# The steps of an expert layer without a copy for changing weights: only the conversion stands in branches

## The chip, the cores and the metric

The kernel runs on one core of a Trainium2 chip. The metric is the time of the whole program on the device in microseconds (us). Three runs of the kernel before gave 1397.78, 1398.32 and 1402.83 us; their median is 1398.32. The profile was taken from one more execution.

The engines are TensorE (PE; its weight loads are listed as PEld), VectorE (DVE), ScalarE (ACT), GpSimd (POOL) and SyncE (SP). Each has its own stream of instructions with its own branches; semaphores order them between engines. A "q" behind an engine's name (PEldq, ACTq) marks what its sequencer does itself: loads of registers, branches, and the issue of transfers.

## The reference, cut to what matters

```python
attn_out = _attn_ref(**attn_kwargs)              # 8 x 8 heads, 576 positions in chunks of 64, softmax per chunk
x = attn_out.transpose(0, 2, 1, 3).reshape(B * S, H * D)     # 4608 tokens x 512
h = np.maximum(x @ w_in, 0.0)                    # dense layer, 512 -> 2048 -> 512
x = (h * h @ w_out).astype(np.float32)
# _moe2_ref: one of 8 experts for each token, 512 -> 1024 -> 512
logits = x @ w_gate + modality_bias[modality_id]
e_idx = np.argmax(logits, axis=1)
probs = softmax(logits)
for e in range(E):
    mask = e_idx == e
    h = np.maximum(x[mask] @ w1[e], 0.0)
    out[mask] = probs[mask, e, None] * (h @ w2[e])
```

All arrays are fp32. The change concerns the last part alone, the layer of experts. With these inputs the router uses two of the eight experts, 2 and 3, for 2325 and 2283 tokens.

## The kernel before, in words

The kernel goes through attention, the dense layer and the layer of experts in one program. It writes each fp32 number as the sum of two f16 numbers (high and low) and leaves out the product of the two low parts, so each matrix product is three matmul passes.

For the layer of experts, the tokens are sorted by expert and cut into pairs of two tiles of 128 tokens; a pair belongs to one expert. There are places for 25 pairs (`PAIRS`); here 19 are used, 0 to 9 for expert 2 and 10 to 18 for expert 3. `NP` is 18 and `EARLY` is 4. Each pair's two matrix products are done by a scheme with seven products of quarter size. `pair1(p)` makes the seven products with w1: 24 matmuls of 128x128 each (L952), into four banks of PSUM in the order a, c, b, a, c, d, a. Each is moved out behind its matmuls by `pair_c`, on ACT (line 90 is the helper of all ACT operations) and DVE (line 93 is the helper of scalar_tensor_tensor). `pair2(p)` makes the seven products with w2: 12 matmuls of 128x256 each (L1018); `pair_o` scales by the gate's weight and `put` (L1044) writes rows of the output by an indirect DMA on POOL. Between its products `pair_s` makes the sums of pair p+1's hidden values for the next `pair2`, split into f16 (L991 to L1003 and L93).

The tokens of a pair come in three operations: `x_gather` (indirect DMA on POOL, L854), `x_tr` (two transposing DMAs, issued from ACT's queue for pairs from 4 on, L862), and `x_sum0` / `x_sum1` (sums by DVE L881, POOL L884 to L887 and L896).

The weights of the current expert stand in SBUF in seven blocks per matrix, each as high and low f16 (`WB`). To make new ones, `load_raw` brings 2 MB of fp32 to the tile `raw` (SP, L773), `presum` scales them on ACT and makes four sums on DVE and POOL (L803), and `conv_part` makes the high part on ACT and the low part on DVE (L824; on POOL for the blocks 2, 4 and 6). Whether a transfer is done is a register's value: with 0 the instruction is issued and moves nothing.

A table of flags in SBUF (`changes`; tiles `chga` and `chgb`) tells for each pair whether its expert is another than that of the pair before. In step p, which is `pair1(p+1)` and then `pair2(p)`, each engine loads a flag to a register and branches. If neither pair p nor p+2 has a new expert, it runs one copy of the step (`fast`); otherwise another (`slow`), which has inside two further choices, between a `first` that converts new w2 between its products and one that doesn't, and likewise a `second` for new w1. So the program of each step holds up to five versions of its halves. In this run the slow copy is taken in steps 8 and 10; new raw weights are loaded in steps 7 and 9, w1 for step 8 and w2 for step 10. Pairs 18 and on may not exist, so the step 17 is inside another branch, `tail`, whose other side is the last `pair2`.

The order of the instructions on each engine is the order in which this code is written.

## Time and profile before

| | |
|---|---|
| median of three runs | 1398.32 us |
| profiled execution | 1397.62 us |
| span in the profile, first to last instruction | 1395.9 us |
| mean granted clock of TensorE | 0.95 |
| TensorE matmul busy | 1231.3 us, 88% of the span |
| VectorE busy | 863.3 us, 62% |
| ScalarE busy | 661.5 us, 47% |
| GpSimd busy | 671.1 us, 48% |

The first matmul of step 2 starts at 953.14 us, the last matmul ends at about 1390 us. So the part which the change touches is some 440 us, the last third of the span. The shares of busy time are means over the whole program; in that third TensorE's are lower.

In a row of the timeline the first number is the start, the second how long the row's instructions took, then the engine, the line, what it writes and reads, how many there are, and in square brackets how long the engine had stood idle before and what released it. "issue" there is time in which the engine waited for nothing that the profile shows.

### The profile page before, as it was taken

What the parts mean: (1) busy time and instruction counts of PE and PEld (TensorE: products, weight loads), DVE (VectorE), ACT (ScalarE), POOL (GpSimd) and SP (SyncE); (2) the same over time, 40 slices, a digit from 0 to 9 for tenths busy, and PEclk for the clock granted to TensorE, in tenths of its full rate; (3) what the DMA queues carried; (4) which work ended last, traced back from release to release, by engine and by line L of the source; (5) the groups of instructions that cost most, each with busy time, mean ns of one, the idle gap of its engine ahead of it and who ended that gap; (6) DMA issues with size and microseconds to landing.
All of it is one profiled execution on the core that took longest, in us unless ns stands there. A gap on an engine that the chain in (4) does not pass through costs nothing. (4 is left out here: it accounts for less than half of the span.)

```text
span 1395.9 us, 30217 instructions
## 1 busy us (share of the span) xinstructions
PE 1231.3 (88%) x12045; PEld 771.2 (55%) x12045; DVE 863.3 (62%) x1787; ACT 661.5 (47%) x1212; POOL 671.1 (48%) x593
## 2 busy tenths in 40 slices
PE   4998999999999999999999987687897745888895
PEld 3444444444444444444444435367787745787784
DVE  6898866746648467474672466765565464655653
ACT  6886644635436345263462443334444344544442
POOL 4476442613416135043250376663665474666664
PEclk9999999999999999999999998889999887999998
DMA  9364323134233232432312043402324315224341
GB/s 373 118 198 126 91 61 92 46 80 73 69 82 63 69 84 52 85 62 61 77 24 46 24 121 91 91 18 62 73 71 132 71 40 87 48 62 80 64 95 34
DMA packets 146161, 115.13 MB, mean 82 GB/s; under 512 B 119770, under 2 KB 119806, under 8 KB 145938
## 3 DMA queue, kind: packets, MB, share of 16 engines
q1 hardware_dynamic: 104514, 83.28, 22.9%
q0 software_dynamic: 7632, 20.54, 4.9%
q10 hardware_dynamic: 33792, 8.39, 4.6%
q8 instruction: 132, 2.16, 0.7%
q14 instruction: 91, 0.75, 0.2%
HBM read 140.10 MB, written 19.80 MB: 115 GB/s over the span
## 5 line engine op out<-in xcount | busy, mean ns | idle before, releaser
L510 PE MATMUL hp<-xtall,big 128*128 128x512 f16 x1728 | 390.6, 383 | 0.0
L525 PE MATMUL op<-big,big 128*128 128x512 f16 x1728 | 387.1, 382 | 0.5 <-POOL big L490 0.5
L525 PEld LDWEIGHTS <-big 128*128 128x128 f16 x1728 | 165.8, 99 | 195.1 <-issue 6.2
L510 PEld LDWEIGHTS <-big 128*128 128x128 f16 x1728 | 165.2, 98 | 194.0 <-issue 8.0
L952 PEld LDWEIGHTS <-big 128*128 128x128 f16 x3192 | 205.3, 106 | 99.5 <-issue 77.3
L490 POOL TENSOR_TENSOR big<-g,big 128x512 f16<-128x512 f32 x144 | 178.3, 1242 | 138.0 <-DVE g L93 94.2
L952 PE MATMUL hq<-big,big 128*128 128x128 f16 x2040 | 142.2, 236 | 86.2 <-issue 29.6
L590 POOL DMA_INDIRECT meta<-mt,di x36 | 37.0, 1027 | 317.2 <-issue 198.1
L93 DVE SCALAR_TENSOR_TENSOR g<-r,bq 128x512 f32<-128x512 f32 x138 | 137.6, 999 | 52.5 <-ACT r L90 44.7
L90 ACT ACTIVATE r<-hp 128x512 f32<-128x512 f32 x138 | 81.8, 593 | 112.9 <-PE hp L510 92.4
L90 ACT ACTIVATE big<-r,bls 128x512 f16<-128x512 f32 x138 | 99.4, 721 | 5.5 <-DVE bls L99 0.6
L1018 PEld LDWEIGHTS <-xtall 128*128 128x128 f16 x840 | 83.8, 100 | 27.0 <-issue 15.5
L1018 PE MATMUL oq<-big,xtall 128*128 128x256 f16 x600 | 74.7, 283 | 12.9 <-DVEq L1376 8.1
L1018 PEld LDWEIGHTS <-ho 128*128 128x128 f16 x756 | 74.9, 100 | 15.4 <-issue 6.0
L90 ACT ACTIVATE xs<-op 128x512 bf16<-128x512 f32 x36 | 21.3, 592 | 122.0 <-PE op L525 122.0
L90 ACT ACTIVATE xtall<-cq 128x512 f16<-128x512 f32 x70 | 42.9, 626 | 66.1 <-DVE cq L93 26.2
L1018 PE MATMUL oq<-big,ho 128*128 128x256 f16 x540 | 65.9, 279 | 5.8 <-DVE oo L93 5.8
L1044 POOL DMA_INDIRECT out_dram<-oo,tib x30 | 34.0, 1135 | 75.6 <-POOLq L1381 42.4
L90 ACT ACTIVATE ho<-cq 128x512 f16<-128x512 f32 x63 | 38.7, 626 | 65.5 <-DVE cq L93 26.2
L90 ACT ACTIVATE big<-hq 128x512 f32<-128x512 f32 x56 | 32.0, 593 | 78.3 <-PE hq L952 32.9
L968 DVE TENSOR_TENSOR cq<-s_all,big 128x512 f32<-128x512 f32 x19 | 13.1, 690 | 79.0 <-ACT big L90 39.5
L90 ACT ACTIVATE ee<-ee 128x512 f32<-128x512 f32 x36 | 22.4, 624 | 78.8 <-DVE ee L332 78.7
(284 smaller groups left out, 1907.7 us busy)
## 6 DMA issues: line engine op xcount, KB each, us to landing
raw<-in_w_dram SPq DMA_DIRECT2D x38, 2048.0 KB
qk<-in_qk_dram SPq DMA_DIRECT2D x36, 512.0 KB
vv<-in_v_dram SPq DMA_DIRECT2D x36, 256.0 KB
x2d<-xs SPq DMA_DIRECT2D x36, 256.0 KB
big<-in_w_in_dram SPq DMA_DIRECT2D x16, 512.0 KB
raw<-in_w_out_dram SPq DMA_DIRECT2D x16, 512.0 KB
raw<-in_w_dram SPq DMA_DIRECT2D x8, 512.0 KB
x2t<-xs SPq DMA_TRANSPOSE x36
```

The source lines that it names most:

```text
L90: nc.scalar.activation(out=out, in_=in_, func=func, **kw)
L93: nc.vector.scalar_tensor_tensor(out=out, in0=in0, scalar=s, in1=in1, op0=op0, op1=op1, **kw)
L490: nc.gpsimd.tensor_tensor(out=lo, in0=q32.rearrange("p (f n) -> p f n", f=nf), in1=hi, op=ALU.subtract)
L510: nc.tensor.matmul(hp[:, q_ * n:(q_ + 1) * n], lhsT=wi[:, la, kk, f * 128:f * 128 + 128], rhs=x[:, lb, kk, :], start=i == 0, stop=i == 3 * ...
L525: nc.tensor.matmul(ps, lhsT=g[:, la, f, t * 128:t * 128 + 128], rhs=wo[:, lb, f, :], start=f == 0 and n == 0, stop=f == KF - 1 and n == 2)
L590: nc.gpsimd.indirect_dma_start(out=meta[:, :], out_offset=bass.IndirectOffsetOnAxis(ap=di[:, 0:1].bitcast(U32), axis=0), in_=mt, in_offset ...
L952: nc.tensor.matmul(ps[:, f * 128:f * 128 + 128], lhsT=WB[0][:, n, la, kk, f * 128:f * 128 + 128], rhs=xa(lb, kk), start=first and f + m + ...
L968: tt(out=c11, in0=bk["b"], in1=SN[0], op=ALU.add)
L1018: nc.tensor.matmul(ps, lhsT=hb[:, la, f * 128:f * 128 + 128], rhs=WB[1][:, n, lb, f, :], start=first and f + m == 0, stop=True, skip_group ...
L1044: nc.gpsimd.indirect_dma_start(out=out[:, :], out_offset=bass.IndirectOffsetOnAxis(ap=t.bitcast(U32), axis=0), in_=o, in_offset=None, boun ...
```

## The change

The step has one version. TensorE's matmuls, and what the other engines do for the tokens, stand in one line of code; between its products are two points. At `point_a`, between the third and fourth product of `pair1(p+1)`, and at `point_b`, between the fourth and fifth product of `pair2(p)`, each engine loads a flag (`gA`, `gB`) and skips the point if nothing is to be done there. Inside stand the conversions alone, under flags of their own: the sums of new w1 at `point_a` of the step in which they were in line before, their conversion at `point_b` of it; the sums of new w2 at `point_b` of the step ahead, their conversion at `point_a`. Behind each point SP issues three conditional loads of raw weights. The table of flags has 13 rows in place of 5. In the tail, the side that goes on behind step 17 is laid out so that the end of the program for 19 pairs comes right behind it.

```diff
@@ -720,20 +720,39 @@
+    ROWS = ("e", "n", "gA", "gB", "sA1", "sA0", "sB0", "sB1", "E1", "E2b", "M1", "E2", "L2")
+
     def changes(n, name):
...
+        put_row("gA", sh[0], sh[2], ALU.max)
+        put_row("gB", sh[1], sh[2], ALU.max)
...
+        put_row("M1", sh[3], t0, ALU.mult)
+        put_row("E2", t0, sh[3], ALU.is_gt)
         return rg
@@ -777,13 +796,13 @@
         load_raw(x, e, part)
 
     def steer(p, row):
-        return mp["rg", int(row == 4 or p >= EARLY)][0:1, row, p:p + 1]
-
-    def late_raw(x, p, which=1):
+        return mp["rg", int(("rg", 1) in mp)][0:1, ROWS.index(row), p:p + 1]
+
+    def late_raw(x, p, row, at):
         if p >= PAIRS:
             return
-        e = nc.sync.value_load(steer(p, 0), min_val=0, max_val=E - 1)
-        need = nc.sync.value_load(steer(p, which), min_val=0, max_val=1)
+        e = nc.sync.value_load(steer(p, "e"), min_val=0, max_val=E - 1)
+        need = nc.sync.value_load(steer(at, row), min_val=0, max_val=1)
         load_raw(x, e, cond=need, cond_hint=False)
 
     def halves(x, v, k):
@@ -826,8 +845,7 @@
     def late_sums(x):
         mp["sums", x] = presum(x, extras(x), [nc.vector, nc.gpsimd, nc.gpsimd, nc.vector])
 
-    def late_both(x):
-        late_sums(x)
+    def late_conv(x):
         for n in range(7):
             conv_part(x, n, mp["sums", x])
 
@@ -1341,106 +1359,103 @@
             fn(*a)
         T = TEND
 
-        def pair1(p, part=range(7), src=None, early=False):
+        def pair1(p, part=range(7), src=None):
             nonlocal T
             for n in part:
                 flush(T)
                 pair_mm1(p, n)
                 if src is not None:
-                    for k in ((0, 1, 2), (3, 4), (5, 6), (), (), (), ())[n] if early else [n]:
+                    for k in ((0, 1, 2), (3, 4), (5, 6), (), (), (), ())[n]:
                         conv_part(1, k, src)
                 pair_c(p, n)
                 T += 1.33
 
-        def pair2(p, part=range(7), s=None, src=None):
+        def pair2(p, part=range(7), s=None):
             nonlocal T
             for n in part:
                 flush(T)
                 pair_mm2(p, n)
-                if src is not None:
-                    conv_part(0, n, src)
                 pair_o(p, n)
-                if s is not None and src is None:
+                if s is not None:
                     pair_s(s, n)
                 T += 1.33
-            if s is not None and src is not None and 6 in part:
-                for n in range(7):
-                    pair_s(s, n)
 
         def branch(p, row):
             on = nc.values_load(steer(p, row), min_val=0, max_val=1)
             return tc.If(on > 0, preferred_fallthrough_block=False)
 
-        def when(p, fn, *a):
-            if p < PAIRS:
-                with branch(p, 1):
-                    fn(*a)
-
-        def both(p, row, yes, no):
-            was = set(gone)
-            with branch(p, row) as cond:
-                yes()
-            after = set(gone)
-            gone.clear()
-            gone.update(was)
-            with cond.Else():
-                no()
-            assert gone == after
-
-        def first(p, src=None):
+        def when(p, row, fn, *a):
+            with branch(p, row):
+                fn(*a)
+
+        def point_a(p):
+            def inner():
+                if p + 1 < PAIRS:
+                    when(p, "sA1", late_sums, 1)
+                when(p, "n", late_conv, 1)
+                if p + 2 < PAIRS:
+                    when(p, "sA0", late_sums, 0)
+
+            when(p, "gA", inner)
+
+        def loads_a(p):
+            late_raw(0, p + 2, "sB0", p)
+            late_raw(0, p + 3, "E1", p)
+            late_raw(1, p + 1, "E2b", p)
+
+        def point_b(p):
+            def inner():
+                if p + 2 < PAIRS:
+                    when(p, "sB0", late_sums, 0)
+                    when(p + 2, "n", late_conv, 0)
+                if p + 1 < PAIRS:
+                    when(p, "sB1", late_sums, 1)
+
+            when(p, "gB", inner)
+
+        def loads_b(p):
+            late_raw(0, p + 3, "M1", p)
+            late_raw(1, p + 2, "E2", p)
+            late_raw(1, p + 1, "L2", p)
+
+        def step(p):
             once(x_tr, p + 2)
-            pair1(p + 1, src=src)
+            pair1(p + 1, range(3))
+            point_a(p)
+            loads_a(p)
+            pair1(p + 1, range(3, 7))
             once(x_gather, p + 3)
             once(x_sum0, p + 2)
-
-        def second(p, src=None):
-            if src is None:
-                pair2(p, range(4), p + 1)
-                late_raw(1, p + 1)
-                late_raw(0, p + 3, 2)
-                once(x_sum1, p + 2)
-                pair2(p, range(4, 7), p + 1)
-            else:
-                pair2(p, range(3), p + 1, src)
-                once(x_sum1, p + 2)
-                pair2(p, range(3, 7), p + 1, src)
-                late_raw(1, p + 1)
-                late_raw(0, p + 3, 2)
-
-        def fast(p):
-            first(p)
-            second(p)
-
-        def slow(p):
-            def new2():
-                late_sums(1)
-                first(p, mp["sums", 1])
-
-            def new1():
-                late_sums(0)
-                second(p, mp["sums", 0])
-
-            both(p, 1, new2, lambda: first(p))
-            late_raw(0, p + 2, 3)
-            if p + 2 < PAIRS:
-                both(p + 2, 1, new1, lambda: second(p))
-            else:
-                second(p)
-
-        def step(p):
-            both(p, 4, lambda: slow(p), lambda: fast(p))
+            pair2(p, range(4), p + 1)
+            point_b(p)
+            loads_b(p)
+            once(x_sum1, p + 2)
+            pair2(p, range(4, 7), p + 1)
+
+        def last(p):
+            def ready():
+                when(p, "sA1", late_sums, 1)
+                late_conv(1)
+
+            when(p, "n", ready)
+            pair2(p)
+
+        def first_change():
+            late_sums(0)
+            late_conv(0)
 
         once(x_gather, 2)
         once(x_gather, 3)
-        pair1(1, src=mp["pre"], early=True)
+        pair1(1, src=mp["pre"])
         once(x_tr, 2)
         once(x_tr, 3)
-        late_raw(0, 2, 2)
+        late_raw(0, 2, "n", 2)
+        late_raw(0, 3, "E1", 0)
         once(x_sum0, 2)
         pair2(0, range(4), 1)
         extras(0)
-        when(2, late_both, 0)
-        late_raw(0, 3, 2)
+        when(2, "n", first_change)
+        loads_b(0)
         once(x_sum1, 2)
         pair2(0, range(4, 7), 1)
         once(x_sum0, 3)
@@ -1450,9 +1465,15 @@
         pair1(2)
         flush(T + 30.0)
         assert not ev
-        when(3, late_both, 0)
-        late_raw(1, 2)
-        late_raw(0, 4, 2)
+
+        def second_change():
+            when(1, "sA0", late_sums, 0)
+            when(3, "n", late_conv, 0)
+            when(1, "sB1", late_sums, 1)
+
+        when(1, "gB", second_change)
+        late_raw(0, 4, "E1", 1)
+        loads_b(1)
         once(x_gather, 4)
         for n in range(7):
             pair_s(2, n)
@@ -1462,15 +1483,13 @@
 
         def tail(p):
             if p == PAIRS - 1:
-                when(p, late_both, 1)
-                pair2(p)
+                last(p)
                 return
-            with tc.If(n_pairs > p + 1 - EARLY) as cond:
+            with tc.If(n_pairs > p + 1 - EARLY, preferred_fallthrough_block=p == NP - 1) as cond:
                 step(p)
                 tail(p + 1)
             with cond.Else():
-                when(p, late_both, 1)
-                pair2(p)
+                last(p)
 
         tail(NP - 1)
```

On ACT, the border between two steps. `cq` holds the quarters of the hidden values, `ho` their f16 parts, `ms` scaled output, `hq` the first products of the next pair. Before:

```order
L90 ACTIVATE ho_11185<-cq_11417 128x512 [waits DVE_49]
L90 ACTIVATE ms<-rq,fsa 128x256 [waits PE_49]
L90 ACTIVATE ho_11186<-cq_11418 128x512 [waits DVE_49]
L90 ACTIVATE ho_11188<-cq_11419 128x512 [waits Pool_49]
L1381 UNCONDITIONAL_BRANCH [waits Activation_sequencer_49]
L1371 TENSOR_LOAD chga
L1381 COMPARE_AND_BRANCH
L862 DMA_TRANSPOSE big_94<-big_94 128x8x128 [waits DMAHW4_49,DMAHW3_49,DMAHW5_49,DMAHW2_49,DMAHW7_49,DMAHW1_49,DMASW2_49]
L862 DMA_TRANSPOSE big_94<-big_94 128x8x128 [waits DMASW3_49]
L90 ACTIVATE big_92<-hq_11390 128x512 [waits PE_49]
```

And now:

```order
L90 ACTIVATE ms<-rq,fsa 128x256 [waits PE_49]
L90 ACTIVATE ho_11196<-cq_11428 128x512 [waits DVE_49]
L90 ACTIVATE ho_11198<-cq_11429 128x512 [waits Pool_49]
L880 DMA_TRANSPOSE big_94<-big_94 128x8x128 [waits DMAHW5_49,DMASW4_49]
L880 DMA_TRANSPOSE big_94<-big_94 128x8x128 [waits DMAHW6_49,DMASW5_49]
L90 ACTIVATE big_92<-hq_11400 128x512 [waits PE_49]
L90 ACTIVATE big_92<-hq_11401 128x512 [waits PE_49]
L90 ACTIVATE xtall<-cq_11427 128x512 [waits DVE_49]
L1384 TENSOR_LOAD chgb
L1388 COMPARE_AND_BRANCH
L1388 UNCONDITIONAL_BRANCH [waits Activation_49,Activation_sequencer_49]
```

The flag and the branch that stood between the last `ho` and the two transposes are gone from there; a flag and a branch now stand behind the first `xtall` of the next pair (point a).

On PE, the border between the last product of `pair2` (`rq`, `oq` of `xtall` here) and the first of the next `pair1` (`hq`). Before:

```order
L1018 LDWEIGHTS xtall
L1018 MATMUL oq_12105<-big_93,xtall 128x256
L1381 UNCONDITIONAL_BRANCH [waits PE_sequencer_49]
L1371 TENSOR_LOAD chga
L1381 COMPARE_AND_BRANCH
L952 LDWEIGHTS big_92 [waits DMAHW3_49,Activation_49]
L952 MATMUL hq_11390<-big_94,big_92 128x128 [waits DVE_49]
L952 LDWEIGHTS big_92
```

And now:

```order
L1036 LDWEIGHTS xtall
L1036 MATMUL oq_12134<-big_93,xtall 128x256
L970 LDWEIGHTS big_92 [waits DMAHW5_49,Activation_49]
L970 MATMUL hq_11400<-big_94,big_92 128x128 [waits DVE_49]
L970 LDWEIGHTS big_92
```

The branch between the two steps is gone, and the weight load of the next pair follows the last matmul.

On PE, between the third product (`s_all`) and the fourth (`hq`) of `pair1`, where nothing but matmuls stood before, there is now:

```order
L970 LDWEIGHTS big_92
L970 MATMUL s_all<-big_94,big_92 128x128
L1384 TENSOR_LOAD chgb
L1388 COMPARE_AND_BRANCH
L1388 UNCONDITIONAL_BRANCH [waits PE_sequencer_49]
L1384 TENSOR_LOAD chgb [waits DVE_49]
L1388 COMPARE_AND_BRANCH
```

The last row is the way past the point; it waits for the engine's own sequencer. The conversion has no matmul, so the skipped code of PE holds flags and branches alone.

## Rows read from the trace of the kernel before

**Rows 1.** Windows by step: start and end, length, busy us of engines, PEclk, DMA.
```profile
982.16:1004.32 22.16, 18.88 (x253) 17.56 (x253) 13.48 (x20) 10.40 (x19) 14.35 (x13) 1.00 0.32 75
1070.74:1103.64 32.90, 22.13 (x252) 20.81 (x253) 16.32 (x23) 11.70 (x21) 16.95 (x15) 0.81 0.51 130
1103.64:1134.18 30.54, 23.16 (x252) 20.76 (x253) 15.06 (x13) 18.20 (x26) 17.94 (x13) 0.86 0.21 40
1134.18:1184.26 50.08, 22.58 (x253) 21.13 (x252) 28.06 (x31) 17.57 (x28) 28.82 (x22) 0.75 0.44 87
1184.26:1205.31 21.05, 20.00 (x252) 18.89 (x253) 17.93 (x17) 12.70 (x20) 14.13 (x10) 0.94 0.10 28
1205.31:1232.85 27.54, 20.36 (x254) 18.91 (x252) 16.48 (x20) 12.26 (x23) 19.49 (x18) 0.94 0.24 59
1232.85:1258.07 25.22, 21.52 (x253) 20.19 (x253) 13.38 (x19) 10.52 (x19) 14.85 (x13) 0.86 0.34 66
1325.63:1348.43 22.80, 20.34 (x252) 19.15 (x253) 13.60 (x20) 10.47 (x20) 14.62 (x13) 0.93 0.31 73
```

**Rows 2.** Timeline of step 12's second half and step 13's start.
```profile
1268.84 2.78 PE L1018 MATMUL oq<-big,ho 128*128 128x256 f16 x24
...
1271.80 1.01 POOL L884 TENSOR_TENSOR big<-big 128x256 f32<-128x256 f32 x1 [1.01 <-DVE big L881]
...
1278.69 1.53 DVE L93 SCALAR_TENSOR_TENSOR cq<-cq,cq 128x512 f32<-128x512 f32 x1
...
1280.26 1.15 ACT L90 ACTIVATE xtall<-cq 128x512 f16<-128x512 f32 x2 [0.57 <-DVE cq L93]
...
1280.29 2.18 PE L952 MATMUL hq<-big,big 128*128 128x128 f16 x36 [2.12 <-DVE cq L93]
...
1281.22 3.45 ACTq L862 DMA_TRANSPOSE big<-big  x2
...
1285.79 2.84 PE L952 MATMUL hq<-big,big 128*128 128x128 f16 x48
...
1291.15 2.02 PE L1018 MATMUL oq<-big,xtall 128*128 128x256 f16 x17
```

**Rows 3.** Branches: duration ns min/median/max, first and last start; all steps, then one border.
```profile
L1381 PEldq COMPARE_BRANCH  x35: 64/2552/5307, 978.3 to 1366.2; - x35
...
L1381 ACTq COMPARE_BRANCH  x2: 34/36/38, 1280.3 to 1281.1; - x2
```
```profile
L1371 ACTq TENSOR_LOAD <-chgb x20: 272/278/290, 982.9 to 1375.6; - x20
...
L1376 PEldq COMPARE_BRANCH  x6: 67/142/309, 917.9 to 1375.8; - x6
```

**Rows 4.** Timeline: three pairs of transposes, and the last pair's first matmul.
```profile
1071.83 7.23 ACTq L862 DMA_TRANSPOSE big<-big  x2
...
1099.70 2.46 ACTq L862 DMA_TRANSPOSE big<-big  x1
...
1211.46 2.65 ACTq L862 DMA_TRANSPOSE big<-big  x2
...
1376.21 5.28 PE L1018 MATMUL oq<-big,xtall 128*128 128x256 f16 x24 [8.06 <-DVEq L1376]
```

**Rows 5.** Conversion of new weights, timeline, then operations that read the raw tile.
```profile
1119.24 3.90 ACT L90 ACTIVATE raw<-raw 128x1024 f32<-128x1024 f32 x4 [2.27 <-DMA raw<-in_w_dram]
...
1125.60 3.36 DVE L803 TENSOR_TENSOR ex<-ex,raw 128x1024 f32<-128x1024 f32 x1 [3.05 <-POOL ex L803]
```
```profile
L90 ACT ACTIVATE big<-raw x8: 1039/1045/1057, 1123.0 to 1196.6; 128x1024 f16<-128x1024 f32 x8
...
L824 POOL TENSOR_TENSOR big<-raw,big x6: 2130/2446/3111, 1127.8 to 1197.7; 128x1024 f16<-128x1024 f32 x6
```

**Rows 6.** Timeline: one operation of the table of flags.
```profile
943.39 0.17 DVE L736 TENSOR_TENSOR chgb<-ndb 1x23 int32<-1x23 f32 x1
```

More of the change, by code (lines that the diff above doesn't have):

```diff
@@ L731, in changes, with put_row @@
         stt(nd[:, 2:n], row[:, 2:n], float(E), nd[:, 2:n], ALU.is_lt, ALU.mult)
[L732 to L736 removed]
+        m = min(n, PAIRS)
+        sh = [nd[:, d:d + m] for d in range(4)]
+        def put_row(name_, a_, b_, op):
+            nc.vector.tensor_tensor(out=rg[:, ROWS.index(name_), 0:m], in0=a_, in1=b_, op=op)
+        nc.vector.tensor_copy(out=rg[:, 1, 0:m], in_=sh[0])
+        put_row("gA", sh[0], sh[2], ALU.max)
+        put_row("gB", sh[1], sh[2], ALU.max)
+        put_row("sA1", sh[0], sh[1], ALU.mult)
+        put_row("sA0", sh[2], sh[0], ALU.is_gt)
+        put_row("sB0", sh[2], sh[0], ALU.mult)
+        put_row("sB1", sh[1], sh[2], ALU.is_gt)
+        put_row("L2", sh[1], sh[2], ALU.mult)
+        t0, t1 = tv[:, 0, 0:m], tv[:, 1, 0:m]
+        nc.vector.tensor_tensor(out=t0, in0=sh[1], in1=sh[2], op=ALU.max)
+        put_row("E1", sh[3], t0, ALU.is_gt)
+        nc.vector.tensor_tensor(out=t1, in0=sh[0], in1=sh[2], op=ALU.is_gt)
+        put_row("E2b", sh[1], t1, ALU.mult)
+        nc.vector.tensor_tensor(out=t0, in0=sh[2], in1=sh[1], op=ALU.is_gt)
+        put_row("M1", sh[3], t0, ALU.mult)
+        put_row("E2", t0, sh[3], ALU.is_gt)
         return rg
```

13 lines of the change are left out of this document (4 added, 9 removed).

## The prediction

> **What bounds the kernel now.** I read the share of busy time first, then the windows by step, then the timeline of one quiet step, then the rows of the branches, and last the timeline of the steps that change weights. TensorE is busy 88% of the span, but not in the part that the change touches. There I call step p the stretch from the first matmul of `pair1(p+1)` to that of the next pair. In a quiet step TensorE is busy 18.88 us of some 22.2 [rows 1]: it is not the bound. What comes back every step is a ring of waits. Call E the moment when `pair2` takes over from `pair1`: 1268.84, and 22.31 us later 1291.15 [rows 2]. From E the DVE adds the halves of the next tokens (L881), POOL makes their sums (from 1271.80, after 1.01 us without work) and then the difference of L999, DVE and ACT make the last split tiles (1278.69, 1280.26), ACT issues the two transposes (1281.22, 3.45 us, and its queue stands still meanwhile), then moves the first product out of PSUM, which frees the bank for the fourth product (1285.79); the fourth to seventh take 5.36 us to the next E. The TensorE gap at the step's start (2.12 us at 1280.29) lies beside this ring, not in it.
>
> Where does that gap come from? The far branch L1381 (fast or slow copy of the step) takes TensorE's sequencer 2.55 us in the median and up to 5.31 [rows 3]. The same kind of branch over a skipped conversion (L1376) takes it 0.07 to 0.31, and ACT's far jump 0.04 [rows 3]. So a far jump is dear on TensorE, where each copy of the step holds some 500 instructions (253 and 253, [rows 1]).
>
> The routing in this run changes expert once in this part: new weights are made in steps 8 and 10 only, and they are loaded in 7 and 9. Steps 7 to 11 take 162.11 us (1070.74 to 1232.85) [rows 1], against 111 for five quiet ones.
>
> **The change, part by part.**
>
> *The ring of a quiet step.* Before, ACT has the step's branch between the last split and the transposes: a first compare at 1280.3, one load of a flag (0.278 us) and a second compare at 1281.1 [rows 2, 3]; the transposes follow at 1281.22. Afterwards no branch stands there; ACT's two branches stand behind the first split of `pair1` and behind the fourth product of `pair2`, where ACT waits for others anyway. I take out 0.85 us (1281.22 less the some 1280.37 at which the queue was free). 22.31 becomes 21.46. The new branches cost each engine a flag load (about 0.3), a compare, and a wait for its own last instruction; the nearest row is the whole cost of the ACT branch just named, 0.85 us, so a point costs between nothing (beside the ring) and 0.85 (in it). I take nothing for ACT and DVE, whose work at those places ends in waits for POOL and TensorE; if the cover is gone on one engine in each step it is +0.85, and the gain of the ring is gone.
>
> *TensorE's far jump.* The median of 2.55 becomes two skips of some 0.14 [rows 3]. That by itself moves nothing, since the ring is late next: the low weights of the first product are written by DVE inside point b in one of its branches, so TensorE now waits at the fifth weight load until DVE has passed that point, behind the stt that makes the fourth quarter (1278.69 plus 1.53, 11.4 after E, [rows 2]). A gap of about 2 us stays there. Such gaps are followed in some steps by the lower clock: the step at 1325.63 has a granted clock of 0.93 and 20.34 us of busy TensorE against 18.88 [rows 1], 1.46 us more, of which the ring hides some. I add 0.25 for the mean step (between 0 and 0.55, five steps of thirteen at 1.46). A quiet step: 21.7.
>
> The Trainium skill (Runtime: NRT & Kernel Launch, section Instruction fetch mechanics) says that a taken branch whose target is outside a window of two blocks of the instruction memory has to fetch it first, and that straight code is fetched ahead nearly free. The trace agrees at both ends (2.55 against 0.14 in the median). By that rule alone one would write the whole 2 us gap of each step down as gain, some 26 us more than I do; that is the rival of the bound by TensorE below.
>
> *Steps 3 to 6* (982.16 to 1070.74, 88.58 us): 4 × 21.7 = 86.8, −1.8; step 2 the same ring, −0.4.
>
> *Steps 12 to 16* (1232.85 to 1348.43, 115.58): 108.5, −7.1. More than in 3 to 6, since step 12 takes 25.22 by the window between the starts and TensorE stands once more inside `pair1` behind an "issue" in steps 12 to 14, which straight code should not do.
>
> *Steps 7 to 11.* Step 7: before, the 2 MB of new weights are loaded from the step's start, and the transposes that ACT issues at 1071.83 take 7.23 instead of 3.45 [rows 2, 4]; then TensorE pays a jump into the slow copy (the step takes 32.90, [rows 1]). Afterwards the load is issued behind point a, which POOL passes at about E, when no transposes are under way, and no copy is jumped into: 21.7. Steps 8 to 10, counted from transposes to transposes, took 111.8 us before (1099.70 to 1211.46, [rows 4]). After the change their conversion is in four portions. Sums: scaling by ACT from 1119.24 to the end of the last DVE sum (1125.60 plus 3.36), 9.7 us. Conversion: seven rounds on ACT of 1.045 = 7.3 us, three low parts on POOL of 2.45 = 7.3, with DVE beside, some 9 us to the last [rows 5]. Sums of w1 at point a of step 8 stand ahead of the outlet of the fourth product; TensorE can go on through the sixth product on banks that are free; E comes 4.5 late (ACT's scaling 3.9 is on its way). Conversion of w1 at point b of step 8 stands fully in the ring, +9.5. Sums of w2 at point b of step 9, +9.7. Conversion of w2 at point a of step 10, +4.5 to E, and the low parts on POOL stand ahead of the next token sums, +4. And 2.8 for the odd gathers and stores that wait behind them on POOL. Together 35 over 3 × 21.7 = 65.1: 100. With all four portions fully in the ring it is 65 + 2 × 9.7 + 2 × 9.5 = 104, with half of each hidden 84. Step 11: 21.7 (27.54 before by TensorE's starts). Sum 21.7 + 100 + 21.7 = 143.4 against 162.1: −18.7, with ends at −35 and −15.
>
> *The end.* The last `pair2` waits 8.06 us before its first matmul at 1376.21 [rows 4], after two jumps, into the tail's other copy and over it. Afterwards the code stands right behind step 17, so it starts when DVE has passed the short branch; by the quiet step DVE is through with a pair some 14.5 after E, and `pair2` ends 9.3 after it, so 5.2 of the wait stay and 2.9 go. The last store still waits for the landing of the one before: −2.5.
>
> *The table of flags* gets ten more DVE operations on one partition at 0.17 each [rows 6], +0.5 of 1.7 since TensorE has matmuls there; below nothing it cannot go, nothing is taken out. SP gets six conditional loads a step instead of two or three; nobody waits for SP in a quiet step, so nothing.
>
> Sum: 0.5 − 0.4 − 1.8 − 18.7 − 7.1 − 2.5 = −30.0. The profiled execution took 1397.62 us, 1.7 more than its span of 1395.9; 1397.6 − 30 = 1367.6. The median of the runs is 0.7 above the profiled one, so 1368.3.
>
> **The rivals.**
>
> *A. Quiet steps stay as they are* (branches at the points put back what leaving ACT's branch out of the ring gives). For it: each not-taken branch empties an engine's queue, and POOL has only 1.01 us without work in the ring [rows 2]. Against: ACT and DVE wait near both points. Then 3 to 6 give nothing, 12 to 16 give 4, steps 7 to 11 17.7: −24, 1374.
>
> *B. The change of weights is not cheaper.* Sums at point a stand ahead of DVE's and ACT's work of the same pair, in order; before, one of the two conversions ran beside the products. Then steps 8 to 10 stay at 111.8 instead of 100, and it is 1380; with A at once 1386.
>
> *C. TensorE becomes the bound.* If nothing gates the first product, a quiet step falls to 18.9 busy plus a little, 19.5: twelve steps × 2.2 = −26 more, 1342. Against: the low weights' wait, and the transposes that are issued only at the ring's pace.
>
> *D. The other side: the skips are not short.* If each of the two points costs TensorE what the far jump does (2.55 us median), and the one before the fourth product is wholly in the ring, a quiet step is 21.7 + 2.55 = 24.3, 2 us longer than before; over 14 steps with the start +36 against the sum's quiet terms, and the two points of the weights' steps likewise, some 8. 1368 + 36 + 8 = 1412. It decides from about 2 us a step upward (14 × 2.1 = 29). For it: a branch in straight code is still a branch, and there are now two on each engine in every step. Against: L1376's 0.07 to 0.31 us over a whole conversion.
>
> **How the numbers follow.** Forecast 50%, A 16%, B 14% (alone or with A), C 8%, D 12%. A measurement of this kernel tells about 0.5%, 7 us, from no change: faster is under 1391.3, slower over 1405.3. All of the forecast, A and C are faster, and nearly all of B; of D, which has smaller sizes too, a good half is slower and the rest within: faster 0.84, same 0.08, slower 0.08. The range: the forecast's own is 1352 to 1378 (swap −35 to −15, quiet steps ± 0.6 × 12); with A and B it reaches 1392, and leaves out C and D: 1351 to 1392.
>
> **What would show it.** Right: the transposes of quiet steps 21.4 to 22.0 apart, issued within 0.1 us of the last split's start, TensorE's branches all under 0.5 us, its gap at the step's start about 2 us behind DVE and not behind "issue"; no transposes of 7 us in step 7; 95 to 105 us from the transposes of step 8 to those of 11. Wrong: quiet steps over 22.3 with ACT, POOL or TensorE behind a branch (A, D), under 20 (C), or more than 110 us between the transposes of step 8 and step 11 (B).

## The result, and the profile after

The changed kernel takes 1360.44 us (median of four runs, 1359.67 to 1362.63) against 1399.26 for the kernel before: a ratio of 0.9721, 95% interval 0.9699 to 0.9744. Timed again later it gave 0.9755 (0.9724 to 0.9787). Forecast were 1368 us and a range of 1351 to 1392. The profiled execution took 1359.67 us with a span of 1357.8.

The page's busy times, as in the table of before:

```profile
PE 1221.4 (90%) x12045; PEld 762.1 (56%) x12045; DVE 856.6 (63%) x1805; ACT 660.8 (49%) x1212; POOL 676.3 (50%) x593
```

TensorE has the same 12045 matmuls and is busy 10 us less; POOL, DVE and ACT do the same work within 7 us. So some 28 of the 38 us are waits of TensorE that went, and 10 are the same matmuls at a higher clock (mean granted clock 0.958 after, 0.950 before). Where they went is read from the transposes, which come once a step:

| stretch (transposes to transposes) | before | forecast | after |
|---|---|---|---|
| start of the program to step 2 | 959.4 | +0.5 | 961.9 (+2.6) |
| steps 2 to 6 | 112.5 | −2.2 | 102.5 (−10.0) |
| step 7 | 27.9 | −6.2 | 20.4 (−7.5) |
| steps 8 to 10 | 111.8 | −11.8 | 106.9 (−4.8) |
| steps 11 to 16 | 137.7 | −7.9 | 122.4 (−15.3) |
| step 17 to the end | 46.7 | −2.5 | 43.7 (−3.0) |

The start moves between executions: a second profile of the same kernel has 957.4 there, so its +2.6 is no cost of the change that could be told.

A quiet step, from one E (1241.63) to the next (1262.16), in the timeline of the changed kernel (the answer to [rows 2]; lines have moved: L999 is L1017, L1003 is L1021, L896 is L914, L862 is L880):

```profile
1241.63 2.78 PE L1036 MATMUL oq<-big,ho 128*128 128x256 f16 x24
...
1248.22 1.71 POOL L1017 TENSOR_TENSOR cq<-cq,cq 128x512 f32<-128x512 f32 x1
...
1249.97 0.69 DVE L1021 TENSOR_TENSOR cq<-cq,cq 128x512 f32<-128x512 f32 x1 [1.16 <-POOL cq L1017]
...
1250.68 2.72 POOL L914 TENSOR_TENSOR big<-big 128x512 f16<-128x512 f32 x2 [0.74 <-POOLq L1388]
...
1250.69 1.69 DVE L93 SCALAR_TENSOR_TENSOR cq<-cq,cq 128x512 f32<-128x512 f32 x1
...
1250.80 0.39 PE L970 MATMUL hq<-big,big 128*128 128x128 f16 x4
...
1252.48 1.26 ACTq L880 DMA_TRANSPOSE big<-big  x1
...
1252.49 2.63 PE L970 MATMUL hq<-big,big 128*128 128x128 f16 x44 [1.30 <-DVEq L1388]
...
1253.84 1.29 ACTq L880 DMA_TRANSPOSE big<-big  x1
...
1256.79 2.85 PE L970 MATMUL hq<-big,big 128*128 128x128 f16 x48 [0.33 <-PEq L1388]
...
1262.16 2.02 PE L1036 MATMUL oq<-big,xtall 128*128 128x256 f16 x17
```

Three things are to be seen. The transposes are issued 0.10 us behind the end of the last stt (scalar_tensor_tensor on DVE, 1250.69 plus 1.69), where before it was 1.00, and they take 2.66 us for the two. DVE's L1021 takes 0.69 us; in the kernel before L1003 took 1.62 or 1.63 in 15 of 16 steps (ns min/median/max, with one ahead of the steps):

```profile
L1003 DVE TENSOR_TENSOR cq<-cq,cq x17: 678/1628/1633, 957.3 to 1367.0; 128x512 f32<-128x512 f32 x17
```

And TensorE waits, behind its first four matmuls, 1.30 us for DVE's way past point b, then once more 0.33 for its own branch of point a, and in no place for ACT: the ring now goes from E through DVE to TensorE's first product, and through all seven products. Its length is 20.53 us here.

TensorE's branches (as in [rows 3]; ns min/median/max):

```profile
L1388 PEldq COMPARE_BRANCH  x84: 64/169/323, 953.7 to 1331.1; - x84
```

No far jump is left in the steps; one of 3.87 us (L1488) comes at the end of the program, when TensorE has no more matmuls to start. The windows by step, columns as in [rows 1]: steps 8, 9, 10 and 13, each from the end of TensorE's wait at the fifth weight load to the next such end.

```profile
1084.81:1117.34 32.53, 20.64 (x252) 18.05 (x252) 17.41 (x22) 14.91 (x23) 18.27 (x15) 0.94 0.23 51
1117.34:1151.25 33.91, 23.10 (x252) 21.39 (x253) 20.42 (x21) 13.50 (x23) 22.63 (x16) 0.76 0.37 110
1151.25:1191.74 40.49, 25.12 (x253) 22.80 (x253) 25.46 (x24) 22.48 (x34) 29.35 (x19) 0.75 0.13 28
1232.11:1252.49 20.38, 18.89 (x252) 17.60 (x252) 13.32 (x18) 10.22 (x20) 14.65 (x14) 1.00 0.34 80
```

The quiet steps 3 to 6 and 11 to 16 all stand at a granted clock of 1.00, the higher of TensorE's two levels, with the 18.9 us of busy TensorE that [rows 1] show for such a step.

Where new weights are made, in the timeline:

```profile
1117.24 9.29 POOL L843 TENSOR_TENSOR big<-raw,big 128x1024 f16<-128x1024 f32 x3 [3.97 <-ACT big L90]
...
1128.14 2.51 PE L970 MATMUL hq<-big,big 128*128 128x128 f16 x22 [5.87 <-POOL big L914]
...
1162.14 2.08 PE L970 MATMUL hq<-big,big 128*128 128x128 f16 x18 [5.94 <-POOL big L914]
```

TensorE stands 5.87 and 5.94 us for POOL's token sums (L914). On POOL these lie behind its three low parts of the conversion, or behind the sums of new weights (L822). In step 7 and at the end, against [rows 4]:

```profile
1064.41 1.27 ACTq L880 DMA_TRANSPOSE big<-big  x1
...
1065.78 2.36 ACTq L880 DMA_TRANSPOSE big<-big  x1
...
1336.09 4.06 PE L1036 MATMUL oq<-big,xtall 128*128 128x256 f16 x24 [3.65 <-DVEq L1388]
```

The transposes of step 7 took 3.73 us together instead of 7.23, and the last pair's first matmul waits 3.65 us instead of 8.06.

### The profile page after: what moved, and what is told of

It is laid out like the page before. It is cut to its first block, busy times and chain, and to the rows that moved or that the text cites. A ratio compares the mean times of both kernels' runs of the same rounds, so it can differ in the third digit from the quotient of the medians.

```text
span 1357.8 us, 31418 instructions
## 1 busy us (share of the span) xinstructions
PE 1221.4 (90%) x12045; PEld 762.1 (56%) x12045; DVE 856.6 (63%) x1805; ACT 660.8 (49%) x1212; POOL 676.3 (50%) x593
## 5 line engine op out<-in xcount | busy, mean ns | idle before, releaser
L525 PEld LDWEIGHTS <-big 128*128 128x128 f16 x1728 | 165.6, 99 | 194.4 <-issue 4.8
L510 PEld LDWEIGHTS <-big 128*128 128x128 f16 x1728 | 164.7, 98 | 193.2 <-issue 6.5
L970 PEld LDWEIGHTS <-big 128*128 128x128 f16 x3192 | 197.1, 103 | 71.1 <-issue 46.3
L590 POOL DMA_INDIRECT meta<-mt,di x36 | 36.7, 1020 | 317.3 <-issue 199.2
L970 PE MATMUL hq<-big,big 128*128 128x128 f16 x2040 | 134.6, 227 | 56.8 <-ACT big L90 17.4
L90 ACT ACTIVATE r<-hp 128x512 f32<-128x512 f32 x138 | 81.8, 593 | 111.2 <-PE hp L510 90.7
L90 ACT ACTIVATE ee<-ee 128x512 f32<-128x512 f32 x36 | 22.5, 624 | 79.4 <-DVE ee L332 79.3
L914 POOL TENSOR_TENSOR big<-big 128x512 f16<-128x512 f32 x36 | 51.8, 1459 | 9.1 <-POOLq L1388 8.3
```

Of the source, the lines that this page charges most:

```text
L90: nc.scalar.activation(out=out, in_=in_, func=func, **kw)
L510: nc.tensor.matmul(hp[:, q_ * n:(q_ + 1) * n], lhsT=wi[:, la, kk, f * 128:f * 128 + 128], rhs=x[:, lb, kk, :], start=i == 0, stop=i == 3 * ...
L525: nc.tensor.matmul(ps, lhsT=g[:, la, f, t * 128:t * 128 + 128], rhs=wo[:, lb, f, :], start=f == 0 and n == 0, stop=f == KF - 1 and n == 2)
L590: nc.gpsimd.indirect_dma_start(out=meta[:, :], out_offset=bass.IndirectOffsetOnAxis(ap=di[:, 0:1].bitcast(U32), axis=0), in_=mt, in_offset ...
L914: eng.tensor_tensor(out=sl[:, 2 * h:2 * h + 2], in0=s[h], in1=sh[:, 2 * h:2 * h + 2], op=ALU.subtract)
L970: nc.tensor.matmul(ps[:, f * 128:f * 128 + 128], lhsT=WB[0][:, n, la, kk, f * 128:f * 128 + 128], rhs=xa(lb, kk), start=first and f + m + ...
```

## The experiments

The numbers of the runs. "Quiet" is the mean distance of the transposes; the whole time is of one execution beside one of the kernel before on the same chip, or the median of four where a ratio stands.

| run | quiet, steps 3 to 5 | quiet, 11 to 16 | steps 8 to 10 | time | before, same chip |
|---|---|---|---|---|---|
| before | 22.2 | 23.0 | 111.8 | 1397.6 | |
| after | 20.5 | 20.4 | 106.9 | 1359.7 | |
| before, transposes first | 22.3 | 22.9 | 115.9 | 1399.8 | 1393.0 |
| before, POOL held | 21.5 | 22.0 | 111.1 | 1381.0 | 1393.0 |
| before, both | 21.0 | 23.0 | 114.0 | 1391.6 | 1393.0 |
| after, far jump back | 24.7 | 25.2 | 111.2 | 1426.2 | 1393.0 |
| after, small block never taken | 20.5 | 20.5 | 108.9 | 1369.3 | 1395.4 |
| after, token sums ahead of b | 22.1 | 22.1 | 104.1 | 1380.2 | 1395.4 |
| after, new weights on DVE alone | 21.8 | 21.8 | 98.4 | 1365.9 | 1395.4 |
| after, b earlier | 19.9 | 20.2 | 107.7 | 1352.3 | 1395.4 |
| b earlier, branch ahead of transposes | 22.5 | 21.9 | 109.3 | 1383.5 | 1396.3 |
| b earlier, timed | 20.4 | 20.1 | 107.0 | 1356.8, 0.9727 | 1395.5 |
| b earlier, one low part on POOL | 20.4 | 19.9 | 99.2 | 1347.0, 0.9650 | 1395.5 |

**Transposes first, in the kernel before.**

```diff
         def step(p):
+            once(x_tr, p + 2)
             both(p, 4, lambda: slow(p), lambda: fast(p))
```

> The kernel before, with one line moved: the two transposes of a step are issued ahead of the step's branch. Quiet steps of the kernel before are 22.3 us (22.0 to 22.8), of the changed kernel 20.3. Theory 1 (three causes: ACT's branch out of the transposes' path, some 0.9 us; POOL's branch that keeps L896 off DVE's L1003, some 0.6; the far jump of TensorE gone, the rest): the transposes are issued some 0.1 us behind the last stt instead of 1.0, and the quiet steps fall by 0.5 to 0.9 to about 21.5. Theory 2 (the far jump of TensorE alone sets the quiet step; the transposes are late only because TensorE is): quiet steps stay at 22.2 to 22.4.

Quiet steps stayed at 22.3. That looks like theory 2, but the edit was a poor one, as the timeline of this run shows:

```profile
1023.74 3.00 ACTq L862 DMA_TRANSPOSE big<-big  x2
...
1028.58 1.61 PE L952 MATMUL hq<-big,big 128*128 128x128 f16 x26 [1.24 <-ACT big L90]
```

ACT's branch now stands behind the transposes and still ahead of the eviction that frees the fourth product's bank; TensorE waits 1.24 us for it. The branch was moved along this path, not out of it. The run decides nothing between the theories. In its steps 12 to 16 TensorE waits for ACT only once, 0.56 us, and they are no shorter: there something else sets the step, as the next run shows.

**POOL held, in the kernel before.** A tiny copy that reads DVE's result:

```diff
                 late_raw(0, p + 3, 2)
+                nc.gpsimd.tensor_copy(out=keep("scr", lambda: const.tile([128, 1], F32, name="scr")), in_=cbuf()[0][:, 0:1])
                 once(x_sum1, p + 2)
```

> The kernel before, with one tiny POOL copy that reads the result of DVE's L1003, put ahead of L896: POOL can't start L896 before L1003 is done, as the branch of point b holds it in the changed kernel. Theory 1: L1003 takes 0.69 us instead of 1.63, the stt behind it starts 0.9 earlier, and quiet steps fall by some 0.6 to about 21.7. Theory 2: L1003 gets shorter, but quiet steps stay at 22.2 to 22.4.

```profile
1020.28 0.69 DVE L1003 TENSOR_TENSOR cq<-cq,cq 128x512 f32<-128x512 f32 x1 [1.84 <-POOL cq L999]
...
1021.04 0.70 POOL L1401 COPY scr<-cq 128x1 f32<-128x1 f32 x1 [0.79 <-DVE cq L1003]
...
1021.71 2.71 POOL L896 TENSOR_TENSOR big<-big 128x512 f16<-128x512 f32 x2
```

L1003 takes 0.69 us in all 16 steps, and quiet steps are 21.5 in the steps 3 to 5. Theory 1 has its 0.7; by one copy the kernel before gains 12 us, in one execution of each on the same chip.

What is left of a quiet step here is TensorE's own, as its branches and matmuls at the start of step 5 show:

```profile
L1381 PEldq COMPARE_BRANCH  x2: 76/1747/3418, 1019.5 to 1023.3; - x2
```
```profile
1019.95 1.47 PE L1018 MATMUL oq<-big,xtall 128*128 128x256 f16 x12
...
1023.48 2.85 PE L952 MATMUL hq<-big,big 128*128 128x128 f16 x48 [2.05 <-DVE ho L93]
...
1027.50 2.84 PE L952 MATMUL hq<-big,big 128*128 128x128 f16 x48
```

The far jump starts 1.95 us ahead of the end of the last matmul and takes 3.42 us; a flag and a short second branch follow, and the first product starts 0.59 us behind the jump's end. The fourth product (1027.50) waits for nothing. In the steps 3 to 7 and 12 to 16 the first product starts 0.58 to 0.66 us behind the jump's end, whatever name stands behind the gap (DVE's `ho`, `oo`, `xtall`, or "issue"): the name is that of an operation that ended about then. No step of these waits for ACT. So with POOL held, a quiet step is its matmuls and the jump's 2.0 to 2.5 us, and in steps 12 to 14 some 0.6 more behind an "issue".

The trace of the kernel before, read the same way, has the jump in each of these steps too: the first product comes 0.58 to 0.60 us behind its end, and the jump takes 3.29 to 3.77 us. The branches at the start of step 14 ([rows 2]), and two of TensorE's waits from step 11 to 16 (in total, times, longest):

```profile
L1381 PEldq COMPARE_BRANCH  x2: 76/1780/3483, 1276.2 to 1280.2; - x2
```
```profile
PE hq L952 <- issue: 6.2, 4, 1.9
PE hq L952 <- ACT big L90: 3.4, 1, 3.4
```

The 3.4 for ACT are in step 11. Behind the jump TensorE waits for ACT at the fourth product in steps 3, 4 and 6 (1.28, 1.14, 0.90 us), stands behind an "issue" in steps 12 to 14 (1.78, 1.23, 1.31), and waits for nothing in steps 5, 15 and 16, which run partly at the lower clock (0.92 to 0.93, 20.3 us of busy TensorE).

**Both edits together.**

> Both edits in the kernel before: the transposes ahead of the branch, and the tiny POOL copy ahead of L896. Theory 1: quiet steps fall by the sum, 1.2 to 1.5, to about 20.9, and what stays against the changed kernel's 20.3 is the far jump's. Theory 2: 22.2 to 22.4. If they give less together than one alone, TensorE's gap at the step's start has become the bound.

21.0 in the steps 3 to 5, as theory 1 has it, but 23.0 in the steps 11 to 16, no better than before. What takes it back is on TensorE: from step 12 on it waits for no other engine. Its gaps behind the jump are 1.9 to 3.0 us, in steps 12 and 13 it stands 2.24 and 0.98 more behind an "issue", and the clock of the steps 12 to 15 is 0.85 to 0.94. Step 12, columns as in [rows 1] (step 4 has 18.72 us of busy TensorE at 1.00):

```profile
1222.36:1248.18 25.82, 21.65 (x253) 20.35 (x253) 12.27 (x19) 10.44 (x19) 14.78 (x15) 0.87 0.36 64
```

So the last sentence of what was expected holds, with the jump as the gap's cause; against POOL held alone (21.5 and 22.0) the edit on ACT shows no gain on the whole.

**The far jump back in the changed kernel,** and the same branch with a short block:

```diff
             once(x_tr, p + 2)
+            def never():
+                for _ in range(3):              # the short one: pair_mm1(p + 1, 0) alone
+                    for n in range(7):
+                        pair_mm1(p + 1, n)
+            if p + 1 < PAIRS:
+                when(p, "sA1", never)
             pair1(p + 1, range(3))
```

> The changed kernel with a branch at the start of each step, behind the issue of the transposes, over a block of some 1000 TensorE instructions that is never taken in this run: TensorE's far jump comes back, and nothing else of the old step. Theory 1: the jump takes 2.5 us or more on TensorE again, and since the first three products are in the ring now, quiet steps rise from 20.3 by 1 to 2.5, to 21.3 to 22.8, and the total by 15 to 35 us; the transposes take 3.4 instead of 2.65 if it is the fetch of the code that slows them. Theory 2: quiet steps go back to 22.3 wholly, the total to about 1385.

> The changed kernel with the same never-taken branch at the start of each step as in the run with the far jump, but its block has 48 TensorE instructions, not 1000. It tells the jump's length from the branch itself. Theory 1 (the length of the jump costs, by code that has to be fetched): TensorE's branch takes 0.1 to 0.4 us, quiet steps are 20.3 to 21.3 against 24.5 with the long block. Rival (the branch itself costs, since the way past a block with matmuls waits for TensorE's last matmul, whatever the block's length): 23.5 to 24.5.

TensorE's branches in the run with the long block, and its first product behind one:

```profile
L1388 PEldq COMPARE_BRANCH  x94: 64/174/4371, 977.4 to 1327.9; - x94
```

```profile
1012.44 0.84 PE L970 MATMUL hq<-big,big 128*128 128x128 f16 x10 [4.23 <-issue]
```

And with the short block:

```profile
L1388 PEldq COMPARE_BRANCH  x98: 64/169/314, 977.9 to 1298.3; - x98
```

A branch over some 1000 instructions takes 3.3 to 4.37 us, the same branch over 48 at most 0.31; a quiet step 24.7 against 20.5, the program 57 us more. So it is the length. 24.7 is above what either theory gave, and even more than before the change: the way past a block that holds matmuls waits for TensorE's last matmul first (the jump starts 0.19 us behind its end), so that the whole jump lies open (4.23 us without work), where in the kernel before it began 1.95 us ahead of TensorE's end (a gap of 2.12, [rows 2]). Behind the gap the granted clock of a step falls to 0.93. In seven of the ten quiet steps the transposes take 2.7 to 2.9 us, so the long jump alone does not make them 3.4. The short block costs nothing in a quiet step; the 10 us more of its one execution lie in steps 2 and 6 (2.8), the steps with new weights (2.0), the end (3.4) and the rest.

**Token sums ahead of point b.**

```diff
+            once(x_sum1, p + 2)
             point_b(p)
             loads_b(p)
-            once(x_sum1, p + 2)
```

> The changed kernel with the token sums on POOL (L914) ahead of point b instead of behind it. Theory 1: in quiet steps L914 runs beside DVE's L1021 again, which takes 1.6 us instead of 0.69, and quiet steps rise from 20.3 to about 20.9. In the steps that change weights TensorE no longer waits 5.9 us twice for L914 behind POOL's part of the conversion: steps 8 to 10 fall from 106.9 to some 97 to 102. Rival: the quiet steps don't care for L1021 (20.3), or POOL's branch isn't what held L914 back (L1021 stays 0.69).

```profile
1242.04 2.71 POOL L914 TENSOR_TENSOR big<-big 128x512 f16<-128x512 f32 x2
...
1242.11 1.63 DVE L1021 TENSOR_TENSOR cq<-cq,cq 128x512 f32<-128x512 f32 x1 [1.84 <-POOL cq L1017]
...
1245.41 1.85 PE L970 MATMUL hq<-big,big 128*128 128x128 f16 x27 [2.40 <-DVEq L1388]
```

L914 starts directly behind L1017 again, L1021 starts 0.07 us after it and ends 0.55 us after L914's first operation. It lost 0.94 us; quiet steps lost 1.6, more than twice what I expected. The rest is in part the clock: TensorE's gap at the start grew from 1.30 to 2.40 us, and some of the steps behind such gaps run partly at the lower level:

```profile
1222.50:1245.40 22.90, 20.35 (x252) 19.24 (x252) 14.71 (x19) 10.40 (x20) 14.72 (x13) 0.93 0.28 71
```

20.35 us of busy TensorE at 0.93, against 18.9 at 1.00. The steps with new weights fell by 2.8 only, to 104.1, where 97 to 102 were expected.

The Trainium skill (SBUF — State Buffer, section SBUF: two separate sides) says that DVE, with two inputs from SBUF, and a GpSimd operation that reads SBUF share a pair of ports, that whoever starts first has it for its whole instruction, and that the other waits. The trace agrees roughly: L1021 ends 0.55 us behind the POOL operation that began 0.07 us ahead of it, a little less than its own 0.69.

**New weights on DVE alone.**

```diff
...
-        mp["sums", x] = presum(x, extras(x), [nc.vector, nc.gpsimd, nc.gpsimd, nc.vector])
+        mp["sums", x] = presum(x, extras(x), [nc.vector] * 4)
...
-            conv_part(x, n, mp["sums", x])
+            conv_part(x, n, mp["sums", x], low=nc.vector)
```

> The changed kernel with the sums and low parts of new weights on DVE alone, not shared with POOL (the early conversion of expert 2's weights stays shared). Theory: DVE and POOL slow each other (DVE 1.21 us alone, 2.1 to 3.4 beside POOL; POOL 2.1 to 3.1), so DVE needs some 8.5 us for seven low parts against 9.3 shared, and POOL goes straight on to the token sums that TensorE waits for: steps 8 to 10 fall from 106.9 to 95 to 101, quiet steps stay 20.3. Rival: the work is bound by their sum, steps 8 to 10 stay at 105 to 110.

```profile
1121.47 1.22 DVE L843 TENSOR_TENSOR big<-ex,big 128x1024 f16<-128x1024 f32 x1
...
1128.29 2.51 PE L970 MATMUL hq<-big,big 128*128 128x128 f16 x22 [1.50 <-POOL big L914]
...
1208.01 2.72 POOL L914 TENSOR_TENSOR big<-big 128x512 f16<-128x512 f32 x2
...
1208.09 1.63 DVE L1021 TENSOR_TENSOR cq<-cq,cq 128x512 f32<-128x512 f32 x1 [1.85 <-POOL cq L1017]
```

The steps 8 to 10 fell to 98.4, as expected: a low part takes DVE 1.22 us alone, and TensorE's wait for L914 is 1.50. The quiet steps did not stay: 21.8, with L1021 at 1.63. In a quiet step nothing of a conversion runs; what changed is only the way past point b. With no POOL work in the skipped block POOL needn't wait there for its own last instruction, L914 follows L1017 at once, and DVE loses its ports. POOL's waits at the branches, in the changed kernel and in this one:

```profile
L1388 POOLq EVENT_SEMAPHORE  x68: 17/17/17, 946.7 to 1343.6; - x68
```
```profile
L1388 POOLq EVENT_SEMAPHORE  x30: 17/17/17, 944.0 to 1350.2; - x30
```

So what keeps them apart in the changed kernel is, by this run, that wait; the last run puts it to a test of its own.

**Point b one product earlier,** in one execution, and then in four beside four of the changed kernel:

```diff
-            pair2(p, range(4), p + 1)
+            pair2(p, range(3), p + 1)
             point_b(p)
             loads_b(p)
+            pair2(p, range(3, 4), p + 1)
             once(x_sum1, p + 2)
```

> The changed kernel with point b one product earlier, behind the third product of pair2 instead of the fourth, so that DVE has passed it before the next pair's first product is due. If TensorE's wait of 1.0 to 1.3 us at the fifth weight load for DVE's pass is in the ring: quiet steps fall from 20.3 to 19.9 or 20.1 (the second product then waits for L914, which ends 11.8 us after E). If the transposes or POOL bound them anyway: 20.3.

> The changed kernel with point b one product earlier, timed: quiet steps 19.8 us, 0.967 of the kernel before (0.965 to 0.969), some 7 us under the changed kernel.

> The changed kernel once more, on the same chip as the next two: 0.972 of the kernel before, quiet steps 20.3 us, steps 8 to 10 107 us.

```profile
1243.07 2.84 PE L970 MATMUL hq<-big,big 128*128 128x128 f16 x48
...
1248.38 1.84 PE L970 MATMUL hq<-big,big 128*128 128x128 f16 x30 [1.12 <-ACT big L90]
```

The next pair's first products run through, and TensorE waits for ACT behind the transposes instead (1.12 us at the fourth product). Quiet steps fall to 19.9 and 20.2 in the first execution. In the timed one the whole is not told apart from the changed kernel: 0.9727 (0.9685 to 0.9768) against 0.9755 (0.9724 to 0.9787).

**A branch ahead of the transposes,** where the kernel before had it, in the kernel with the earlier point b:

```diff
+            scr = keep("scr", lambda: const.tile([128, 1], F32, name="scr"))
+            if p + 1 < PAIRS:
+                when(p, "sA1", act, scr, ms[:, 0, 0:1])
             once(x_tr, p + 2)
```

> The kernel with point b one product earlier, and a never-taken branch over one tiny ACT operation between the last split of a step and the transposes, where the kernel before had its branch. In the kernel without it TensorE waits 0.9 to 1.2 us for ACT behind the transposes in each quiet step, so the ring runs through ACT. If ACT's branch costs what the prediction took out (0.85 us): the transposes are issued 0.9 to 1.4 us later behind the last stt, and quiet steps rise from 19.8 to 20.6 or 21.2. If something else hides it: 19.8 to 20.0.

```profile
1008.82 3.29 ACTq L880 DMA_TRANSPOSE big<-big  x2
...
1012.80 1.39 PE L970 MATMUL hq<-big,big 128*128 128x128 f16 x22 [1.85 <-ACT big L90]
...
1027.09 1.53 DVE L93 SCALAR_TENSOR_TENSOR cq<-cq,cq 128x512 f32<-128x512 f32 x1
...
1030.13 1.26 ACTq L880 DMA_TRANSPOSE big<-big  x1
```

Here the ring runs through ACT, and the branch costs more than I had said: the transposes are issued 1.51 us behind the end of the stt (1028.62), and they take 3.29 us instead of 2.66. Quiet steps are 22.5 and 21.9 against 19.9 and 20.2. So without the far jump ACT's branch at this place is in the ring. For the kernel before this run shows nothing; there TensorE waited for ACT in three of the nine steps 3 to 6 and 12 to 16. Why transposes that are issued later take longer is not shown.

**Both improvements.** As on DVE alone, with point b earlier, and with `low=nc.gpsimd if n == 4 else nc.vector`:

> Point b one product earlier, and new weights' sums and low parts on DVE, but for the low part of block 4, which stays on POOL. If it is the wait of POOL on its way past point b for its own last instruction (there only while the skipped block holds POOL work) that keeps L914 off L1021: L1021 takes 0.69 us, quiet steps stay at 19.8 as in the run before, and steps 8 to 10 fall from 107 to 95 to 101: 0.960 of the kernel before (0.957 to 0.964). If the hold comes from something else that the run on DVE alone took away: L1021 1.63, quiet steps 20.5 to 21.5, 0.97 to 0.98.

```profile
1238.52 0.69 DVE L1021 TENSOR_TENSOR cq<-cq,cq 128x512 f32<-128x512 f32 x1 [1.85 <-POOL cq L1017]
...
1238.98 2.81 POOL L914 TENSOR_TENSOR big<-big 128x512 f16<-128x512 f32 x2 [0.50 <-POOLq L1388]
```

One POOL operation in the skipped block is enough: L914 starts 0.50 us behind POOL's branch, L1021 takes 0.69 in all 16 steps, quiet steps are 19.9 in the steps 11 to 16, and the steps 8 to 10 take 99.2. The time is 1347.0 us, 0.9650 of the kernel before (0.9618 to 0.9683), where the changed kernel on the same chip has 0.9755 and the one with point b earlier 0.9727: it beats both. The 0.957 to 0.964 that were expected were just missed.

## Why the prediction was right, and where its sizes were off

The direction, the range and the places were right; the sum was 8 us short, and two terms were off to opposite sides, by some 16 and 7 us. That the whole came out within 8 us is in part luck: the two cancel, and what shortened the quiet step was not what the prediction named. Of its signs three did not come: the transposes of most quiet steps are 20.1 to 20.6 us apart, not 21.4 to 22.0; the gap behind DVE is 1.0 to 1.5 us, not about 2; and steps 8 to 10 took 106.9 us, not 95 to 105.

*The quiet step, 21.7 forecast, 20.4 to 20.5 measured:* some 16 us over the steps 2 to 7 and 11 to 16. The prediction had the ring go through ACT, with the far jump beside it ("by itself moves nothing"). That is the step that failed. Its ring was read from [rows 2], which show the second half of step 13 and the start of step 14 (not 12 and 13). There the fourth product (1285.79) stands without an idle time: it waits neither for ACT nor for the transposes. What TensorE waits for besides the jump lies earlier:

```profile
1283.79 0.83 PE L952 MATMUL hq<-big,big 128*128 128x128 f16 x12 [1.31 <-issue]
```

So the 22.31 us are 18.9 of matmuls, 2.12 behind the far jump, and 1.31 behind an "issue". The jump's 2.55 us, the median of [rows 3], also counts the short second branches; in the quiet steps it takes 3.29 to 3.77. The wait for ACT ended last in three of nine quiet steps only, and it is gone when POOL is held, with ACT's branch still in its place.

The runs show three causes in its place. First, POOL: I read its 1.01 us without work as a danger, and a branch on POOL as a cost between nothing and 0.85. It was a gain of 0.94 on DVE's L1021, since POOL's wait holds L914 off DVE's ports; the trace of before had the 1.63 of L1003 beside L896 in it, and I did not ask what it would be alone. Held in the kernel before, POOL takes the quiet step from 22.2 and 23.0 to 21.5 and 22.0 (steps 3 to 5 and 11 to 16). Second, the far jump: with POOL held, its gap of 2.0 to 2.5 us is TensorE's only wait in most steps, and in the changed kernel 1.0 to 1.5 behind DVE and some 0.3 at point a stand in its place (20.5 and 20.4). A long jump put back there costs 4.2 us a step, more than in the kernel before, since it starts only behind the last matmul. Third, the clock: behind the shorter gaps these quiet steps stay at the higher level, so the 0.25 for the lower one was not due. The steps 12 to 14 lost their "issue", as said.

ACT's branch was taken away as said (the transposes come 0.90 us earlier behind the stt, forecast 0.85), but no run shows that this alone gains anything in the kernel before. It had to go with the jump: put back without the jump, in the kernel with point b earlier, it costs some 2 us a step. What the changed kernel would be with ACT's branch alone put back was not run. The transposes take 2.66 instead of 3.45 us; that is measured, why is open, and TensorE does not wait for them in the changed kernel's quiet step.

*Steps 7 to 10.* Step 7 came as worked out (20.4 for 21.7, no transposes of 7 us). Steps 8 to 10 took 106.9 for 100: over three quiet steps of 20.4 they cost 45.7 us, where the forecast had 35. Sums and conversion were sized by POOL's 2.45 us an operation, but the three low parts took 9.29 us one behind the other and beside DVE, and the token sums queue behind them. The forecast had 4 us for this in step 10, and 2.8 for gathers and stores; TensorE waited 5.87 us for the token sums in step 9 and 5.94 in step 10. With these waits at 1.50 and 1.38, on DVE alone, the three steps take 98.4. The forecast also had no term for the clock there: TensorE is busy 20.6, 23.1 and 25.1 us at 0.94, 0.76 and 0.75, against 18.9. How much of that lies behind other waits is not shown. From the transposes of step 8 to those of step 9 it was 36.7 us (35.7 by the forecast's terms), then 30.6; the loss is in step 10, 39.7.

*The end:* −3.0 for −2.5, the first matmul's wait fell from 8.06 to 3.65. *The table of flags:* not told apart from the scatter of the start.

*The rivals.* A (quiet steps as before) and B (new weights not cheaper) did not come, though B was near: −4.8 of −11.8. C, TensorE as the bound at 19.5, is nearly reached by the kernel with point b earlier (19.7 to 20.0 in steps 11 to 15), not by the change. D, long skips: TensorE's skips took 0.17 us in the median; the run with the far jump shows what D would have been (24.7 us and 1426, where D had 24.3 and 1412).

## What to carry to other kernels

A branch cost TensorE by the length of what it jumped over (3.3 to 4.4 us over some 1000 instructions, at most 0.31 over 48), so give rare work a small block of its own and leave the matmuls in one line. A wait's name in a trace can be that of an operation that only ended about then: the far jump stood behind DVE's name, and what gave it away was its constant distance from the next matmul, step by step. A ring of waits is re-read after each edit: ask of every operation in it how long it takes alone, because a neighbour that starts a little later can give back more than the edit itself. Operations of two inputs that read SBUF on DVE and POOL at the same time made each other wait: in step 8, seven low parts on DVE alone took 9.0 us, four and three side by side 10.5.

## What the runs showed of the hardware that was not expected

- A branch's way past a block waited for POOL's last instruction only where the block held POOL work (68 waits in the changed kernel, 30 with new weights on DVE alone). This was worth 0.94 us of DVE's time a step (0.69 against 1.63), and taking the last POOL operation out of a block that never runs in those steps cost 1.4 us in each.
- TensorE's branch over some 1000 instructions took 3.3 to 4.37 us, over 48 at most 0.31, on ACT, DVE and POOL branches took at most 0.06 in the same program.
- In the changed kernel's quiet steps a gap of 1.0 to 1.5 us ahead of the first product left the granted clock at 1.00; in steps with 1.9 to 3.0 us, in the runs with token sums ahead of b and with DVE alone, it fell to about 0.93 in some and stayed at 1.00 in others.
